# A small load of u moved from the first features' step to the head of the constants (RWKV-6 attention with a hard-swish MLP)

## The chip, the cores and the metric

One core of a Trainium2 chip runs the kernel. The metric is the device time of one execution in microseconds, as the median of several runs. The profile shows one execution; its span is shorter than that execution's time by what lies around it.

## The reference, cut to what matters

Two blocks follow each other. The first is a linear attention with a state that decays: for each batch and head, over 768 steps,

```
cur   = (u * k_t) outer v_t
y_t   = r_t . (state + cur)
state = w_t * state + k_t outer v_t
```

with r, k, v, w of shape (4, 8, 768, 48) and u of shape (8, 48). The part of y that u makes is a number per step and head, the sum over the head's 48 elements of r u k, times v_t. The second block takes y as x of shape (3072, 384): h = x @ w_in, g = h * clip(h + 3, 0, 6) / 6, out = g @ w_out, with w_in of (384, 2048) and w_out of (2048, 384). The weights come as float64.

## The kernel before, in words

**Tiling.** Each sequence is cut into chunks of 128 steps; a chunk i of all 8 heads is one unit of the attention, and there are 24 of them. Every chunk has a chain of steps, each a short function: its features (r, k and w, with 112 partitions of heads' elements) are loaded (feat), two scans on VectorE make the running products of w (back, fore), k and r are scaled by them (K, R), TensorE makes the scores and reads and writes the state (score, read, kv), and ScalarE copies results out of PSUM (kvs, leave). Four chunks make a block of the MLP, whose products (up, down) take most of TensorE's time. The weights are loaded in 16 tiles of 768 KB (fetch, L397), and ScalarE and VectorE turn each from float64 into float32 (low L406, sign L411, shift L417, full L421).

**What u is for.** For the first nine chunks (BY_PE) the diagonal of the scores comes from TensorE: own (L467, VectorE) multiplies r and k into a tile rk, dot (L479, TensorE) multiplies it with u_col, a tile of 112 x 8 numbers that holds u, sum (L485, ScalarE) copies the result to dg, and diag0 and diag1 (L495, ScalarE) put it on the diagonal of A. dot of chunk i is called dot0, dot1 and so on below. rk has one buffer, so the next chunk's own waits for this chunk's dot.

**The order of the work.** It is written out by hand. A planner holds all steps with engine, duration and needs, but their order is a string (ORDER) that gives each step its place, and each engine runs its own in that order. The durations only decide, in a small model inside the plan, how many fillers are put between TensorE's steps of the first 60 us: a filler (spin, L1276) is a product of the identity with itself whose result nobody reads.

TensorE's start reads: 14 fillers (28 matmuls in the profile, which counts two passes for each), dot0, 2 fillers (4), the transposes of K of chunk 0 (turn0, L520), 9 fillers (18), the write of the state (kv0, L620), the scores (L504), dot1, the clearing of y (L674), 7 fillers (14), and the read of chunk 0. turn0 needs a PSUM bank that is free again when sum0 has copied dg; kv0 needs kn of chunk 0 (L528) and its values (v_in).

**Queues.** All loads but one go out from SP: the first weight tile, then w of chunk 0 (260 KB), its r and k (512 KB), the features of chunk 1 (772 KB), the values of chunk 0, the second weight tile, the values of chunk 1, the third weight tile, and the features of chunks 2 and 3. Eight loads at a time can be in flight: each load takes one of eight semaphores in turn, and the ninth waits until the first has landed. The one load that doesn't go out from SP is that of u_col, 112 x 8 floats, 3.5 KB: load_feat(0) issues it on ScalarE's queue (L354), so it stands there behind the table load and the low and sign of the first weight tile.

Of the kernel before, what the change touches and what calls it, by code (L numbers as in the profile page):

```python
# [16 lines left out]
ACT = mybir.ActivationFunctionType  # L17
# [8 lines left out]
BC = 4  # L26
# [220 lines left out]
def fast_path(tc, feat, tok, wflat, ub, ug, moe_w_in, moe_w_out, out, flag, n_chunks):  # L247
# [5 lines left out]
    nc = tc.nc  # L253
# [16 lines left out]
    with ExitStack() as ctx:  # L270
# [17 lines left out]
        plan = Plan()  # L288
# [12 lines left out]
        u_col = const.tile([PR, P, 2], F32, name="u_col")  # L301
# [4 lines left out]

        def constants():

            nc.vector.memset(back, 0.0)
            nc.vector.memset(back[:, :, HL:], 1.0)  # L310
            for b in starts:
                nc.vector.memset(b, 0.0)
            nc.vector.memset(y_ps[:PR, :, P * HL:], 0.0)
            nc.vector.memset(three, 3.0)
            nc.vector.memset(ones, 1.0)
            make_identity(nc, ident)
            nc.gpsimd.tensor_add(eyes, ident[:, :HL], ident[:, HL:])

            mask_f = wk.tile([128, HL], F32, name="clip")
            nc.gpsimd.memset(mask_f, 1.0)  # L320
            for a in range(2):
                nc.gpsimd.affine_select(out=mask_f[a * HL:(a + 1) * HL], in_=mask_f[a * HL:(a + 1) * HL],
                                        compare_op=ALU.is_gt, fill=0.0, base=0, pattern=[[1, HL]], channel_multiplier=-1)
            nc.gpsimd.tensor_copy(out=mask, in_=mask_f)

            for _ in range(4):
                spin()

            new_x(0)
            x3_0 = blocks[0]["x3"]  # L330
            sel = blocks[0]["sel"] = wk.tile([PR, NCC, 128], F32, name="S_", bufs=1)
            nc.gpsimd.memset(x3_0, 0.0)
            nc.gpsimd.memset(sel, 0.0)
            for g in range(2):
                nc.gpsimd.tensor_copy(out=sel[:, :, g * GP + D:g * GP + D + X3],
                                      in_=ident[0:PR, g * GP:g * GP + D].rearrange("q (j r) -> q j r", j=NCC))

        def new_x(bk):

            x = wk.tile([128, NCC + 1, MB], F32, name="xT")  # L340
            blocks[bk].update(xT=x, x3=x[:PR, NCC])
# [7 lines left out]
        def load_feat(i):  # L349
            b = io.tile([feat.shape[1], nf], F32, name="feat_in")  # L350
            a = b[:PR]
            if i == 0:
                nc.sync.dma_start(out=b[:, 2 * n:], in_=feat[chunk_of[i], :, 2 * n:])
                nc.scalar.dma_start(out=u_col, in_=ug)  # L354
            else:
                nc.sync.dma_start(out=b, in_=feat[chunk_of[i]])
            st[i].update(b=b, r=a[:, :n].rearrange("q (x t) -> q x t", t=HL),
                         k=a[:, n:2 * n].rearrange("q (x t) -> q x t", t=HL), w=a[:, 2 * n:])
# [171 lines left out]
        def by_dma(i):  # L530
            return i >= FLIP
# [447 lines left out]
        def do(fn, *args):  # L979
            return lambda: fn(*args)  # L980
# [5 lines left out]
        def when(i):  # L986

            bk, c = divmod(i, BC)
            return BASE[bk] - LAG - (BASE[bk] - BASE[bk - 1]) / BC * (BC - 1 - c) if bk else -99.0
# [8 lines left out]
        def scored(i):  # L998
            return f"score{i}" if i <= BC else f"read{i - 1}"

        def turned_by(i):
            if by_dma(i):
                return f"split{i}"
            return f"turn{i}" if i <= BC + 1 else f"read{i - 2}"
# [4 lines left out]
        def written_by(i):  # L1009
            return f"kv{i}" if i in SOLO else f"read{i - 1}"  # L1010

        for i in range(NT):
            t = when(i)
            k = START[i] if i < len(START) else when(i - 2) - AHEAD
            first, last = is_first(i), is_last(i)
            dve = i < EARLY
            behind = [f"fetch{BEHIND[i]}"] if i < len(BEHIND) and BEHIND[i] >= 0 else []
            plan.add(f"feat{i}", "SP", 0.45 if i else 1.15, do(load_feat, i), behind + [f"feat{i - 1}"] * (i > 0) + ["later"] * (i == 1), k - 20, kb=735 if i else 294,
                     hold=[("feat", [f"K{i}", f"R{i}"] + [f"own{i}"] * (i < BY_PE))])
            plan.add(f"tok{i}", "SP", 0.45, do(load_tok, i), behind + [f"feat{i}"] * (i > 1) + ["later"] * (i < 2), k - 19.9, kb=320,  # L1020
                     hold=[("tok", [read_by(i)])])
# [23 lines left out]
            due = k + 0.7 if i < len(START) else when(i - 1)  # L1045
# [2 lines left out]
                plan.add(f"score{i}", "PE", 0.63, do(score, i), [f"K{i}", f"R{i}"] + [f"score{i - 1}"] * (i > 0), due,  # L1048
                         [("bank", [f"above{i}"])] * 2)
            plan.add(f"above{i}", "DVE", 0.68, do(above, i), [scored(i), f"diag1{i}"], due + 0.5)  # L1050
            if i <= BC + 1:
                plan.add(f"turn{i}", "PE", 0.45, do(turn_k, i), [f"K{i}"] + [f"turn{i - 1}"] * (i > 0), due + 0.01, [("ps", [f"turned{i}"])])
            if by_dma(i):
                plan.add(f"split{i}", "ACT", 0.9, do(split_k, i), [f"K{i}"], due - 6, [("rk", [f"flip{i}"])])
                plan.add(f"flip{i}", "SP", 1.0, do(flip_k, i), [f"split{i}"] + [f"flip{i - 1}"] * by_dma(i - 1), due - 5, [("kvs", [f"turned{i}"])], kb=229)
            plan.add(f"turned{i}", "ACT", 0.8 if by_dma(i) else 0.42, do(turned_k, i), [f"flip{i}" if by_dma(i) else turned_by(i)] + [f"turned{i - 1}"] * (i > 0), due - 2 if i > BC + 1 else due + 0.5,
                     [("kn", [written_by(i)])])
            if i in SOLO:
                plan.add(f"kv{i}", "PE", 0.6, do(write_alone, i), [f"turned{i}", f"tok{i}"], t - 0.2,
# [66 lines left out]
        for f in range(NFC):  # L1126
            for c0, c1 in parts_of[f]:
                m, x = c1 - c0, c0 // BY_SUM
                k = UP[2 * x] + f * UP[2 * x + 1] + (c0 % BY_SUM)
# [35 lines left out]
        for bk in range(NB):  # L1165
            K = BASE[bk]
# [6 lines left out]
            for d in range(2 * (bk > 0)):  # L1173
# [8 lines left out]
                writer, readers, due = {}, {}, {}  # L1182
# [77 lines left out]
        for k, (which, j) in enumerate(vets):  # L1260
            i = 8 + k // 2
# [10 lines left out]
        def spin():  # L1272

            n_ = spins[0] = spins[0] + 1
            at = n_ % 4 * L
            nc.tensor.matmul(still[:, at:at + L], lhsT=ident, rhs=ident, start=n_ == 0, stop=True, skip_group_check=True)  # L1276
# [7 lines left out]
        plan.spin, plan.hint = spin, hint  # L1284
        plan.hint_at = f"down{NB - 1}.1.3.0"
        constants()
        plan.emit()

# [237 lines left out]
def kernel(  # L1526
# [25 lines left out]
    flags = ctx.enter_context(tc.tile_pool(name="flags", bufs=1))  # L1552
    flag = flags.tile([1, 1], I32, name="flag")
    fast_path(tc, feat, tok, wflat, ub, ug, moe_w_in, moe_w_out, out, flag, n_chunks)
    bad = nc.values_load(flag[0:1, 0:1], min_val=0, max_val=128)
    with tc.If(bad > 0, preferred_fallthrough_block=True, label="general"):
# [68 lines left out]
```

## Time and profile before

| | |
|---|---|
| median of 3 runs | 532.97 us (532.53 to 534.28) |
| profiled execution, its own time | 532.08 us |
| its span | 530.3 us |
| TensorE busy | 518.1 us (98%) |
| VectorE busy | 432.5 us (82%) |
| ScalarE busy | 290.4 us (55%) |
| load of u_col: issued, landed after | 5.34 us, 7.05 us |

In the profile PE is TensorE's matmuls, PEld its weight loads, DVE is VectorE, ACT is ScalarE, POOL is GpSimd, SP is SyncE; L12 is line 12 of the kernel before. A timeline row has the start in us, the duration, the engine and line, the operation, the tiles written and read, how many of them, and in brackets the idle time before it with what ended it. The chain of waits is the work that ended last, in order of time: start, duration, what. A DMA row has the issuing queue, how many, the size and the time from issue to landing. Buffer numbers are left out of names: rk of chunk 0 and rk of chunk 1 are both "rk".

### The profile page before, as it was taken

How to read it: one execution, taken by the hardware profiler on the slowest of the kernel's cores; microseconds unless marked ns; L12 is line 12 of the kernel's file. 1: busy time of each engine (PE TensorE's matmuls, PEld its weight loads, DVE VectorE, ACT ScalarE, POOL GpSimd, SP SyncE). 2: the span in 40 equal slices, each digit the busy share in tenths (PEclk: the TensorE clock that was granted, in tenths of full speed). 3: DMA queues.
4: the chain of work that ended last, by engine and by line, in shares of the span. 5: the costliest groups of instructions: out<-in, count | busy, mean ns of one | idle time of the engine just before them, and what ended most of it. 6: DMA issues, size and time to landing. Idle time of an engine off the chain costs nothing.

```text
span 530.3 us, 13609 instructions
## 1 busy us (share of the span) xinstructions
PE 518.1 (98%) x5642; PEld 478.7 (90%) x5642; DVE 432.5 (82%) x762; ACT 290.4 (55%) x680; POOL 86.0 (16%) x79
## 2 busy tenths in 40 slices
PE   4999999999999999999999999999999999999997
PEld 4988889999788999888999988999988999988997
DVE  6699999999799977787996678897789996568951
ACT  2789897445257754587462455665458552334220
POOL 2000000133023043313220503044201300000000
PEclk8899999999999999999999999999999999999999
DMA  8676485035502171454333305433814445453101
GB/s 322 246 297 243 140 284 185 11 90 143 186 2 62 26 199 34 129 183 93 107 99 100 131 20 138 138 100 101 270 33 147 104 151 201 127 197 139 59 11 56
DMA packets 37235, 70.33 MB, mean 133 GB/s; under 512 B 19088, under 2 KB 27184, under 8 KB 37168
## 3 DMA queue, kind: packets, MB, share of 16 engines
q1 hardware_dynamic: 37040, 69.40, 40.7%
q8 instruction: 46, 0.75, 0.6%
q14 instruction: 21, 0.17, 0.1%
q10 hardware_dynamic: 128, 0.00, 0.0%
HBM read 59.69 MB, written 4.72 MB: 121 GB/s over the span
## 4 chain that ended last, share of the span: by engine, by line
PE 88%; DVE 4%; DMA 4%; ACT 2%; SPq 1%; issue 1%; DVEq 0%
PE bank L897 31%; PE bank L840 28%; PE bank L739 7%; PE bankS L897 5%; PE bankS L840 5%; PE y_ps L598 2%; PE bank L504 2%; PE y_ps L607 2%; PE y_ps L620 2%; PE bankS L1276 1%; DMA u_col<-in_ug_dram 1%; DMA feat_in<-in_feat_dram 1%; PE ps L479 1%; DMA bits<-in_moe_w_in_dram 1%; PE ps L520 1%
## 5 line engine op out<-in xcount | busy, mean ns | idle before, releaser
L861 ACT ACTIVATE clip<-g,three 128x512 f32<-128x512 f32 x80 | 56.1, 719 | 49.3 <-DVE g L857 28.2
L857 DVE TENSOR_TENSOR g<-bank,g 128x512 f32<-128x512 f32 x80 | 53.4, 684 | 27.3 <-PE bank L840 23.7
L897 PE MATMUL bank<-w_out,g 128*128 128x192 f32 x384 | 67.4, 327 | 0.0
L897 PEld LDWEIGHTS bank<-w_out,g 128*128 128x128 f32 x384 | 63.3, 190 | 0.5
L865 DVE SCALAR_TENSOR_TENSOR g<-clip,g 128x512 f32<-128x512 f32 x80 | 59.2, 755 | 3.7 <-ACT clip L861 3.7
L495 ACT ACTIVATE A<-eyes,dg 128x64 f32<-128x64 f32 x192 | 49.8, 338 | 0.5 <-DVE dg L487 0.3
L454 POOL TENSOR_TENSOR K<-feat_in,E 112x512 f32<-112x512 f32 x17 | 25.0, 1469 | 151.0 <-DVE E L434 86.9
L855 ACT COPY g<-bank 128x512 f32<-128x512 f32 x50 | 28.8, 585 | 33.5 <-PE bank L840 32.3
L739 PE MATMUL bank<-xT,w_in 128*128 128x256 f32 (+1 forms) x216 | 45.4, 360 | 0.0
L840 PE MATMUL bank<-xT,w_in 128*128 128x256 f32 x160 | 40.2, 379 | 0.3 <-issue 0.3
L739 PEld LDWEIGHTS bank<-xT,w_in 128*128 128x128 f32 x216 | 36.6, 190 | 4.0
L458 POOL TENSOR_TENSOR W<-feat_in,W 112x512 f32<-112x512 f32 x17 | 24.8, 1456 | 94.4 <-DVE W L443 80.8
L706 ACT COPY xT<-y_ps 48x256 f32<-48x256 f32 x88 | 32.2, 366 | 10.4 <-PE y_ps L607 9.5
L915 ACT ACTIVATE o<-bank 128x192 f32<-128x192 f32 x36 | 11.5, 327 | 46.7 <-PE bank L897 46.6
L897 PE MATMUL bankS<-w_out,g 128*128 128x192 f32 x192 | 34.9, 328 | 0.0
L897 PE MATMUL bank<-more,g 128*128 128x192 f32 x192 | 34.3, 329 | 0.0
L840 PEld LDWEIGHTS bank<-xT,w_in 128*128 128x128 f32 x160 | 30.2, 190 | 4.4 <-issue 0.6
L897 PEld LDWEIGHTS bank<-more,g 128*128 128x128 f32 x192 | 31.5, 190 | 0.7
L897 PEld LDWEIGHTS bankS<-w_out,g 128*128 128x128 f32 x192 | 31.6, 190 | 0.2
L470 POOL TENSOR_TENSOR rk<-rk_in 128x384 f32<-128x384 f32 x15 | 17.5, 1164 | 87.2 <-DMA kvs<-rk 39.3
L840 PE MATMUL bank<-xT,bits 128*128 128x256 f32 x120 | 30.7, 380 | 0.0
L443 DVE TENSOR_TENSOR_SCAN W<-feat_in,start 112x520 f32<-112x520 f32 x24 | 30.6, 1273 | 0.0
(306 smaller groups left out, 1128.7 us busy)
## 6 DMA issues: line engine op xcount, KB each, us to landing
feat_in<-in_feat_dram SPq DMA_DIRECT2D x23, 772.5 KB, 5.3
bits<-in_moe_w_in_dram SPq DMA_DIRECT2D x8, 768.0 KB, 6.3
bits<-in_moe_w_out_dram SPq DMA_DIRECT2D x8, 768.0 KB, 5.4
feat_in<-in_moe_w_in_dram SPq DMA_DIRECT2D x8, 768.0 KB, 4.9
feat_in<-in_moe_w_out_dram SPq DMA_DIRECT2D x8, 768.0 KB, 5.3
rk_in<-in_tok_dram SPq DMA_DIRECT2D x15, 384.0 KB, 4.4
v_in<-in_tok_dram SPq DMA_DIRECT2D x24, 192.0 KB, 4.4
feat_in<-in_wflat_dram SPq DMA_DIRECT2D x6, 768.0 KB, 4.7
```

Of the source, the lines that this page charges most:

```text
L443: nc.vector.tensor_tensor_scan(out=W_, data0=d["w"][:, :-1], data1=starts[i % 2].rearrange("q p t -> q (p t)"), initial=0.0, op0=ALU.mult, ...
L454: early(i).tensor_mul(d["K"], d["k"], d["E"][:, :, 1:])
L458: early(i).tensor_mul(d["R"], d["r"], d["R"])
L495: nc.scalar.activation(out=d["A"][:, h, :], in_=eyes, func=ACT.Copy, scale=d["dg"][:, h])
L706: nc.scalar.copy(out=blocks[bk]["xT"][g * GP:g * GP + D, :, at:at + HL], in_=st[i]["y_ps"][a][(g ^ a) * GP:(g ^ a) * GP + D, :, :])
L739: nc.tensor.matmul(h_ps[:, :(c1 - c0) * L], lhsT=w_in[:, f // 2, j, f % 2, :], rhs=b["xT"][:, j, c0 * L:c1 * L], start=(j == 0), stop=(j = ...
L840: nc.tensor.matmul(b["p", d, c][:, z * HB:(z + 1) * HB], lhsT=weight(W_PLACE[r], d)[:, z, :], rhs=x_at(bk, X_PLACE[r]), start=fresh and z ...
L855: nc.scalar.copy(out=out_, in_=src)
L857: nc.vector.tensor_tensor(out=out_, in0=src, in1=out_of(bk, d, other), op=ALU.add if sign > 0 else ALU.subtract)
L861: nc.scalar.activation(out=c, in_=out_of(bk, d, u), func=ACT.Relu, bias=three, scale=twice)
L865: nc.vector.scalar_tensor_tensor(out=g, in0=blocks[bk]["r", d, u], scalar=6.0, in1=g, op0=ALU.min, op1=ALU.mult)
L897: nc.tensor.matmul(b["d", p, to][:, :h], lhsT=a, rhs=w(), start=(f == 0 and k in (1, 5)), stop=(f == HF - 1 and k in (2, 3, 4)), skip_grou ...
```

## The change

The load of u_col becomes the first statement of constants(), which is emitted ahead of all steps, and leaves load_feat. It stays on ScalarE's queue. In the plan the duration of feat0 goes from 1.15 to 0.45, those of split, flip and turned for the later chunks go up a little, and turn is no longer planned for a chunk that is transposed by DMA.

```diff
         def constants():
 
+            nc.scalar.dma_start(out=u_col, in_=ug)
             nc.vector.memset(back, 0.0)
...
             if i == 0:
                 nc.sync.dma_start(out=b[:, 2 * n:], in_=feat[chunk_of[i], :, 2 * n:])
-                nc.scalar.dma_start(out=u_col, in_=ug)
             else:
...
-            plan.add(f"feat{i}", "SP", 0.45 if i else 1.15, do(load_feat, i), behind + [f"feat{i - 1}"] * (i > 0) + ["later"] * (i == 1), k - 20, kb=735 if i else 294,
+            plan.add(f"feat{i}", "SP", 0.45, do(load_feat, i), behind + [f"feat{i - 1}"] * (i > 0) + ["later"] * (i == 1), k - 20, kb=735 if i else 294,
...
-            if i <= BC + 1:
+            if i <= BC + 1 and not by_dma(i):
...
-                plan.add(f"split{i}", "ACT", 0.9, do(split_k, i), [f"K{i}"], due - 6, [("rk", [f"flip{i}"])])
-                plan.add(f"flip{i}", "SP", 1.0, do(flip_k, i), [f"split{i}"] + [f"flip{i - 1}"] * by_dma(i - 1), due - 5, [("kvs", [f"turned{i}"])], kb=229)
+                plan.add(f"split{i}", "ACT", 0.94, do(split_k, i), [f"K{i}"], due - 6, [("rk", [f"flip{i}"])])
+                plan.add(f"flip{i}", "SP", 1.24, do(flip_k, i), [f"split{i}"] + [f"flip{i - 1}"] * by_dma(i - 1), due - 5, [("kvs", [f"turned{i}"])], kb=229)
```

ScalarE's instructions from the start of the program, before and after (the waits name the semaphore of the load that is waited for):

```order
 L1620 UNCONDITIONAL_BRANCH [waits barrier_Pool_Activation_PE_DVE_SP_release]
+L309 DMA u_col<-in_ug_dram 112x8
 L406 ACT_TABLE_LOAD
-L406 ACTIVATE more<-bits 128x768 [waits DMAHW0_49]
-L411 ACTIVATE more<-bits 128x768
-L354 DMA u_col<-in_ug_dram 112x8
+L406 ACTIVATE more<-bits 128x768 [waits DMAHW1_49]
+L411 ACTIVATE more<-bits 128x768
 L461 COPY w_min<-E 112x8 [waits DVE_49]
```

The load moved past the table load and the two conversions of the first weight tile; as it is now the first load of the program, it holds the first semaphore, and the first weight tile the second.

TensorE's instructions around dot0, at the start of the program:

```order
 L1276 MATMUL bankS<-ident 128x128 [waits Pool_49]
 L1276 MATMUL bankS<-ident 128x128 x13
-L479 MATMUL ps<-u_col,rk 64x2 [waits DMAHW4_49,DVE_49]
+L479 MATMUL ps<-u_col,rk 64x2 [waits DMAHW0_49,DVE_49]
 L479 MATMUL ps<-u_col,rk 64x2 x7
 L1276 MATMUL bankS<-ident 128x128 x2
```

Nothing moved here, and the number of fillers is the same all along TensorE's queue; dot0 waits for the same load under another semaphore.

SP's queue from the start of the program, with the chunk's features (feat_in), values (v_in) and weight tiles (bits), after the change:

```order
 L397 DMA bits<-in_moe_w_in_dram 128x768
 L354 DMA feat_in<-in_feat_dram 128x521
 L361 DMA feat_in<-in_feat_dram 128x1024
 L356 DMA feat_in<-in_feat_dram 128x1545
 L368 DMA v_in<-in_tok_dram 128x384
 L397 DMA bits<-in_moe_w_in_dram 128x768
 L368 DMA v_in<-in_tok_dram 128x384
 L397 DMA bits<-in_moe_w_in_dram 128x768 [waits DMAHW0_49]
 L356 DMA feat_in<-in_feat_dram 128x1545 [waits DMAHW1_49]
```

The order of SP's loads and the names in these waits are as before, but the first semaphore is now that of u_col and the second that of the first weight tile, where they were those of the first weight tile and of w of chunk 0.

More of the change, by code (lines that the diff above doesn't have):

```diff
@@ L1050, in fast_path @@
             plan.add(f"above{i}", "DVE", 0.68, do(above, i), [scored(i), f"diag1{i}"], due + 0.5)
-            if i <= BC + 1:
+            if i <= BC + 1 and not by_dma(i):
                 plan.add(f"turn{i}", "PE", 0.45, do(turn_k, i), [f"K{i}"] + [f"turn{i - 1}"] * (i > 0), due + 0.01, [("ps", [f"turned{i}"])])
             if by_dma(i):
-                plan.add(f"split{i}", "ACT", 0.9, do(split_k, i), [f"K{i}"], due - 6, [("rk", [f"flip{i}"])])
-                plan.add(f"flip{i}", "SP", 1.0, do(flip_k, i), [f"split{i}"] + [f"flip{i - 1}"] * by_dma(i - 1), due - 5, [("kvs", [f"turned{i}"])], kb=229)
-            plan.add(f"turned{i}", "ACT", 0.8 if by_dma(i) else 0.42, do(turned_k, i), [f"flip{i}" if by_dma(i) else turned_by(i)] + [f"turned{i - 1}"] * (i > 0), due - 2 if i > BC + 1 else due + 0.5,
+                plan.add(f"split{i}", "ACT", 0.94, do(split_k, i), [f"K{i}"], due - 6, [("rk", [f"flip{i}"])])
+                plan.add(f"flip{i}", "SP", 1.24, do(flip_k, i), [f"split{i}"] + [f"flip{i - 1}"] * by_dma(i - 1), due - 5, [("kvs", [f"turned{i}"])], kb=229)
+            plan.add(f"turned{i}", "ACT", 1.1 if by_dma(i) else 0.42, do(turned_k, i), [f"flip{i}" if by_dma(i) else turned_by(i)] + [f"turned{i - 1}"] * (i > 0), due - 2 if i > BC + 1 else due + 0.5,
                      [("kn", [written_by(i)])])
```

## The prediction

> **What bounds the kernel now.** I read the page's busy shares first, then the chain of waits from the start to 24 us, then the timelines of DVE and ACT over the same stretch, the granted clock by stretches, and last the landing times of single loads. The page's first part says that TensorE is the engine that counts:
>
> ```profile
> PE 518.1 (98%) x5642; PEld 478.7 (90%) x5642; DVE 432.5 (82%) x762; ACT 290.4 (55%) x680; POOL 86.0 (16%) x79
> ```
>
> PE is busy for 518.1 of 530.3 us, so only some 12 us of the span have no matmul in them. The chain of waits (start us, duration us, what) shows that one load of 3.5 KB stands in the largest hole:
>
> ```profile
> 5.34 7.05 DMA u_col<-in_ug_dram
> 12.40 0.14 issue
> 12.53 1.02 PE ps L479 x16
> 13.56 1.16 PE bankS L1276 x4
> 14.71 0.75 PE ps L520 x4
> 15.46 2.72 PE bankS L1276 x18
> 18.18 0.51 PE y_ps L620 x32
> ...
> 19.16 0.56 PE ps L479 x16
> ...
> 20.79 1.56 PE bankS L1276 x14
> ...
> 23.69 0.55 PE ps L520 x4
> ...
> 34.70 0.57 PE y_ps L620 x31
> ```
>
> The load of u is issued at 5.34, lands 7.05 us later, and 0.14 us after that the first products with it (dot0, L479) run. PE's own row of dot0 in the timeline gives the hole (the bracket is the idle time before it):
>
> ```profile
> 12.53 1.02 PE L479 MATMUL ps<-u_col,rk 112*64 112x2 f32 x16 [5.28 <-DMA u_col<-in_ug_dram]
> ```
>
> So PE stands from 7.25 to 12.53. Two more things are in these rows. The same 16 matmuls of L479 take 1.02 us at 12.53 and 0.56 at 19.16; four transposes of L520 take 0.75 at 14.71 and 0.55 at 23.69; 14 fillers of L1276 take 1.56 at 20.79 (0.111 each), while 18 took 2.72 before. The granted clock by stretches says why (stretch, length, busy times, PEclk, DMA share, GB/s):
>
> ```profile
> 7.30:9.90 2.60, 0.00 (x0) 0.00 (x0) 2.29 (x5) 0.23 (x2) 0.00 (x0) 1.00 0.97 371
> 10.00:12.40 2.40, 0.00 (x0) 0.00 (x0) 1.75 (x3) 0.00 (x0) 0.00 (x0) 0.50 1.01 404
> 12.50:16.70 4.20, 4.17 (x31) 4.18 (x32) 2.05 (x3) 2.60 (x10) 0.00 (x0) 0.50 1.00 416
> 17.00:24.00 7.00, 6.91 (x161) 6.26 (x160) 4.74 (x10) 4.50 (x13) 0.00 (x0) 1.00 0.34 132
> ```
>
> The clock fell to 0.50 in the hole and stayed there to about 16.7. The hole costs its own length and then a stretch at half clock.
>
> **The change part by part.**
>
> *The load goes to the head of ACT's queue.* Before, it stood behind the first two conversions, the first of which waits for its weight tile to 5.33 (ACT's rows below). Now ACT issues it first, at about 0.8, where its first instruction is now. What dot0 needs besides u is rk of chunk 0 from DVE:
>
> ```profile
> 7.86 0.69 DVE L467 TENSOR_TENSOR rk<-feat_in 112x512 f32<-112x512 f32 x1 [0.28 <-DMA feat_in<-in_feat_dram]
> ...
> 11.07 0.68 DVE L458 TENSOR_TENSOR W<-feat_in,W 112x512 f32<-112x512 f32 x1
> 13.59 0.69 DVE L467 TENSOR_TENSOR rk<-feat_in 112x512 f32<-112x512 f32 x1 [1.84 <-PE ps L479]
> ...
> 19.26 0.36 DVE L550 TENSOR_TENSOR S<-kvs,w_min 112x192 f32<-112x192 f32 x1 [3.58 <-ACT kvs L631]
> ```
>
> rk is ready at 8.55. Even if u took the same 7.05 us from its new issue it would land at 7.9, so its landing time need not be known: dot0 starts when rk is there, at 8.55 + 0.14 = 8.69. Gain so far 12.53 - 8.69 = 3.84 us.
>
> *The clock.* The hole shrinks from 5.28 to 8.69 - 7.25 = 1.44 us. I take it that the clock stays at full. Then from dot0 to the first write into the state (kv0, L620) PE needs 0.56 + 4 x 0.111 + 0.55 + 18 x 0.111 = 3.56 us, where it took 1.02 + 1.16 + 0.75 + 2.72 = 5.65. Gain 2.09, together 5.93: kv0 at 12.25 in place of 18.18. The trace has no hole of 1.4 us at this place, so the bounds of this term are 0 and 2.09; I take 2.09, since the clock was still at 1.00 to 9.9, 2.6 us into the long hole. The Trainium skill (TensorE: Matmul & The Clock Gate, section HAM oscillation) has the rule that gaps above about 3.4 us make the array fall back to half rate; by that rule a hole of 5.28 falls back, as the trace shows, and one of 1.44 does not, and the sum would be the same 5.93. The same page (Part 1) says that the window is free-running and shifts from run to run; by that some runs would keep only part of the 2.09, which no run here shows yet.
>
> *What is late next, on ACT.* Between dot0 and kv0 ACT must copy dg, build the diagonal and copy kn:
>
> ```profile
> 0.80 1.28 ACT L406 ACT_TABLE_LOAD   x1 [0.80 <-PEq L1611]
> 5.33 1.08 ACT L406 ACTIVATE more<-bits 128x768 uint16<-128x768 uint32 x1 [3.25 <-DMA bits<-in_moe_w_in_dram]
> ...
> 13.59 0.17 ACT L485 COPY dg<-ps 128x8 f32<-128x8 f32 x1 [6.02 <-PE ps L479]
> 13.86 2.02 ACT L495 ACTIVATE A<-eyes,dg 128x64 f32<-128x64 f32 x8
> 15.78 0.51 ACT L528 COPY kn<-ps 128x448 f32<-128x448 f32 x1
> 18.75 0.48 ACT L631 COPY kvs<-y_ps 112x384 f32<-112x384 f32 x1 [2.46 <-PE y_ps L620]
> 19.13 1.08 ACT L406 ACTIVATE more<-bits 128x768 uint16<-128x768 uint32 x1
> ```
>
> dg starts 0.04 after dot0's end (12.53 + 1.02), so at 9.29, and kn ends 15.78 + 0.51 - 13.59 = 2.70 later, at 11.99: 0.26 before PE asks. ACT is then free for kvs, which follows PE and ends at 19.23 - 5.93 = 13.30. The table load now stands behind the issue of u; an issue takes 0.47 in SP's row below, so it ends near 2.6 instead of 2.1. The first conversion waits for its tile to 5.33, so this edit costs nothing; its cover is 2.7 us.
>
> *On DVE.* The scaled r (L458) is ready at 11.75 and doesn't move. rk of chunk 1 no longer waits 1.84 for dot0's bank and starts at 11.75, if its features are there. That load, issued between 2.1 and 2.5, took 7.5 us:
>
> ```profile
> feat_in<-in_feat_dram SPq DMA_DIRECT2D x1, 772.5 KB, 7.5
> ```
>
> It lands by 10.0, so rk is ready at 12.44, before dot1 at 19.16 - 5.93 = 13.23. The scan and reciprocal of chunk 1 follow it; DVE was done with them at 19.26 - 3.58 = 15.68, now 1.84 earlier, at 13.84, which is after kvs: the state's first step (L550) starts at 13.84, 5.4 us earlier, not 5.9. PE reads that state behind its 14 fillers, at 22.35 before and 16.4 now, so the 0.5 us are hidden.
>
> *Loads that keep their time.* The first burst of loads is bound by bandwidth (404 and 416 GB/s above) and lands when it did. The tightest is the second weight tile, for the conversion at 19.13, now due at 13.20:
>
> ```profile
> 3.36 0.47 SPq L397 DMA_DIRECT2D bits<-in_moe_w_in_dram  x1
> ```
>
> ```profile
> bits<-in_moe_w_in_dram SPq DMA_DIRECT2D x1, 768.0 KB, 9.7
> ```
>
> 3.36 + 9.7 = 13.06: just in time.
>
> Later loads are issued when a buffer comes free, so they move with the engines. The one without slack is the values of chunk 2, issued between 28.5 and 28.8, which land some 0.1 before PE starts with them (34.70, in the chain above):
>
> ```profile
> v_in<-in_tok_dram SPq DMA_DIRECT2D x1, 192.0 KB, 6.0
> ```
>
> *SP's queue.* Its order is the same, but its eighth load waits for a semaphore that u now holds, and its ninth for that of the first weight tile: both go out a little earlier. They stand behind six loads of the same queue that are in flight until 13, so they land as before: nothing. The changed durations in the plan's table change no instruction's place and no number of fillers: nothing.
>
> **The sum.** 3.84 + 2.09 = 5.93 us. From kv0 on every engine is in the same relation as before, and PE has no waits of size until the end, so I carry it to the end whole. The profiled execution took 532.08 (span 530.3, and 1.8 around it), which makes 526.2; the median of the runs is 0.9 above it, so from 532.97 it makes 527.0.
>
> **The rivals.**
> *The clock falls anyway* (0.12). The stretch around the hole is too idle and PE runs the next one at half rate. Against: the hole is a quarter of the old. For: the shares at which the clock turns aren't in this trace. Then only the waiting goes: 532.97 - 3.84 = 529.1.
> *The loads set the pace* (0.09). The fifth weight tile is now asked for while the first burst still runs (DMA share 1.00 to 16.7), and pushes the values of chunk 2 back by one tile, 786 KB at 416 GB/s = 1.9 us. For: that load has no slack. Against: DMA share is 0.34 between 17 and 24. Gain 4.0, 529.0.
> *Nothing is left* (0.04). The same load keeps its old landing time of 34.6 whatever is issued when, and PE waits there for all that it won: 533.0. Against: its issue is chained to ACT's conversions, which move.
> *Slower* (0.03). The table load, now behind the DMA, is held up by the burst of loads. If it ended at T, two conversions of 1.08, the copy of dg (0.2), the transposes (0.75) and 18 fillers at half clock (2.72) would follow, and kv0 would be at T + 5.8: from T = 12.4 on that is later than 18.18. The longest landing in the burst, of a load issued between 5.9 and 6.2, is this one:
>
> ```profile
> feat_in<-in_feat_dram SPq DMA_DIRECT2D x1, 772.5 KB, 11.3
> ```
>
> With it T = 1.2 + 11.3 + 1.3 = 13.8, kv0 at 19.6, 1.4 slower and 534.4; held up somewhat longer, it passes the bound. Against: the table load took 1.28 before, beside SP's first issue.
>
> **How the numbers follow.** The forecast has 0.72, 527.0. A measurement of this kernel can tell about 0.3%, 1.6 us, from no change. The first two rivals are faster by more than that too: faster 0.72 + 0.12 + 0.09 = 0.93, same 0.04, slower 0.03. The range goes from 525.8 (the profiled execution's 526.2, less 0.4 for sums of rounded rows) to 529.8 (the first two rivals, and 0.7 for a clock that returns later still).
>
> **What would show it.** Right: u issued before 1.3 us; PE's idle time before dot0 near 1.4 and ended by DVE's rk, not by a DMA; the clock at 1.00 between 8.7 and 17; 16 matmuls of L479 in about 0.56 at 8.7; kv0 near 12.3; L620 of chunk 2 near 28.8. Wrong: u landing after 8.6; a clock of 0.50 after 8.7 (first rival); idle time before L620 of chunk 2, ended by the values' load (second and third); a table load that ends after 5.3 (slower).

## The result, and the profile after

The changed kernel takes 529.69 us (median of nine runs, 527.37 to 531.58); the kernel before took 533.46 beside it (nine runs, 532.53 to 534.60). The ratio is 0.9924, 95% interval 0.9904 to 0.9944: faster by 3.8 us, where 5.9 were forecast. The profiled execution took 528.87 with a span of 527.1, 3.2 less than that of before.

The busy shares hardly differ from those of before, as a change of 4 us in 530 must look there; the start is where to look. Timelines of ACT and DVE of the kernel after (start, duration, engine and line, tiles), and the row of its load of u:

```profile
0.81 0.42 ACTq L309 DMA_DIRECT2D u_col<-in_ug_dram  x1
1.25 1.28 ACT L406 ACT_TABLE_LOAD   x1 [1.25 <-PEq L1611]
...
11.20 0.51 ACT L528 COPY kn<-ps 128x448 f32<-128x448 f32 x1
...
12.96 1.07 ACT L406 ACTIVATE more<-bits 128x768 uint16<-128x768 uint32 x1
```

```profile
7.61 0.67 DVE L467 TENSOR_TENSOR rk<-feat_in 112x512 f32<-112x512 f32 x1
...
11.40 0.69 DVE L467 TENSOR_TENSOR rk<-feat_in 112x512 f32<-112x512 f32 x1
...
13.39 0.31 DVE L550 TENSOR_TENSOR S<-kvs,w_min 112x192 f32<-112x192 f32 x1
```

```profile
u_col<-in_ug_dram ACTq DMA_DIRECT2D x1, 3.5 KB, 4.7
```

u lands at 0.81 + 4.7 = 5.5, before rk is there. PE's timeline of the kernel after, first around dot0 and kv0, then around the write of chunk 2 (kv2, the second L620):

```profile
8.33 0.63 PE L479 MATMUL ps<-u_col,rk 112*64 112x2 f32 x16 [0.93 <-DVE rk L467]
8.89 0.71 PE L1276 MATMUL bankS<-ident 128*128 128x128 f32 x4
...
9.83 2.19 PE L1276 MATMUL bankS<-ident 128*128 128x128 f32 x18
11.95 0.57 PE L620 MATMUL y_ps<-v_in,kn 64*48 64x48 f32 x32
...
27.03 1.45 PE L682 MATMUL bank<-xT,S__117 112*128 112x64 f32 x12
29.52 0.57 PE L620 MATMUL y_ps<-v_in,kn 64*48 64x48 f32 x32 [1.03 <-ACT xT L689]
...
30.59 1.51 PE L1276 MATMUL bankS<-ident 128*128 128x128 f32 x6
31.89 2.59 PE L739 MATMUL bank<-xT,w_in 128*128 128x256 f32 x6
```

kv0 starts at 11.95, 6.2 us earlier. But 17 us on there is a hole of 1.03 that before did not have, and behind it the same 6 matmuls of L739 that need 1.46 us elsewhere (a row of a later run, below) take 2.59. The granted clock by stretches of the kernel after (stretch, length, busy times, clock, DMA share, GB/s) says why:

```profile
6.90:10.20 3.30, 2.37 (x33) 2.16 (x32) 3.27 (x6) 1.89 (x7) 0.00 (x0) 1.00 1.02 408
...
17.00:24.00 7.00, 7.00 (x151) 6.64 (x148) 6.58 (x12) 5.94 (x14) 0.00 (x0) 1.00 0.81 305
...
27.40:30.70 3.30, 2.27 (x59) 2.09 (x59) 3.27 (x8) 3.25 (x10) 0.00 (x0) 1.00 0.99 393
30.80:34.10 3.30, 3.30 (x12) 2.78 (x11) 1.11 (x2) 0.64 (x4) 0.00 (x0) 0.50 0.99 403
34.30:40.00 5.70, 5.70 (x61) 4.92 (x60) 5.14 (x11) 5.48 (x13) 0.00 (x0) 1.00 0.34 117
```

The clock held in the smaller hole ahead of dot0 and fell at 30.8 instead, for one stretch. The DMA share between 17 and 24 is 0.81, where it was 0.34 before: the next weight tile is asked for at 16.91 instead of 22.84, while the first burst still runs (its last load lands at 21.15). The rows of the two loads that SP issues at 22.1 and 22.6, of u once more as a broadcast over partitions (u_bc, used from chunk 9 on) and of chunk 2's values:

```profile
u_bc<-in_ub_dram SPq DMA_DIRECT2D x1, 192.0 KB, 6.7
v_in<-in_tok_dram SPq DMA_DIRECT2D x1, 192.0 KB, 6.8
```

The values are issued at 22.60, 6.0 us earlier than before, and take 6.8 us where they took 6.0, so they land at 29.4, 0.14 before kv2. Over their flight the DMA share is 0.90, where it was 0.82 (a stretch of after, then one of before):

```profile
22.60:29.40 6.80, 5.79 (x84) 5.04 (x83) 6.77 (x13) 6.57 (x20) 0.00 (x0) 1.00 0.90 306
28.60:34.60 6.00, 5.86 (x84) 5.11 (x84) 5.97 (x11) 5.89 (x18) 0.00 (x0) 1.00 0.82 294
```

Pairing the matmuls of the two traces one by one, fillers left out, gives how far PE is ahead of the kernel before along the program:

| at (us, before) | ahead by (us) | what happened since the row above |
|---|---|---|
| 12.53, dot0 | 4.20 | the wait for u is gone |
| 18.11, kv0 | 6.16 | full clock from dot0 to kv0 |
| 34.70, kv2 | 5.18 | hole ahead of kv2 |
| 37.62, L739 | 3.59 | half clock behind it |
| 64.71 | 3.84 | steps of about 0.2 and less |
| 135.51, L840 | 2.99 | one new wait, below |
| 526.63, last | 3.21 | |

The wait at 135.51 is in PE's row of the kernel after, and the kernel before has none there:

```profile
132.52 1.10 PE L840 MATMUL bank<-xT,bits 128*128 128x256 f32 x4 [0.84 <-DMA xT<-xT]
```

### The profile page after: what moved, and what is told of

It reads as the page before. It is cut to its first block, busy times and chain, and to the rows that moved or that the text cites. A ratio compares the mean times of both kernels' runs of the same rounds, so it can differ in the third digit from the quotient of the medians.

```text
span 527.1 us, 13608 instructions
## 1 busy us (share of the span) xinstructions
PE 517.7 (98%) x5642; PEld 477.7 (91%) x5642; DVE 431.6 (82%) x762; ACT 290.1 (55%) x680; POOL 86.7 (16%) x79
## 4 chain that ended last, share of the span: by engine, by line
PE 86%; DVE 6%; DMA 3%; SPq 2%; ACT 1%; issue 1%; DVEq 0%
PE bank L897 29%; PE bank L840 28%; PE bank L739 8%; PE bankS L897 5%; PE bankS L840 5%; PE y_ps L598 2%; PE bank L504 2%; PE y_ps L607 2%; PE y_ps L620 2%; DMA feat_in<-in_feat_dram 1%; PE bankS L1276 1%; PE ps L479 1%; DMA bits<-in_moe_w_in_dram 1%; SPq L713 1%; DVE E L434 1%
## 5 line engine op out<-in xcount | busy, mean ns | idle before, releaser
L739 PE MATMUL bank<-xT,w_in 128*128 128x256 f32 (+1 forms) x216 | 46.7, 366 | 0.0
L739 PEld LDWEIGHTS bank<-xT,w_in 128*128 128x128 f32 x216 | 37.4, 194 | 4.5 <-issue 0.3
L840 PE MATMUL bank<-xT,w_in 128*128 128x256 f32 x160 | 40.1, 379 | 0.0
L840 PEld LDWEIGHTS bank<-xT,w_in 128*128 128x128 f32 x160 | 30.2, 190 | 3.8
L434 DVE TENSOR_TENSOR_SCAN E<-feat_in,back 112x520 f32<-112x520 f32 x24 | 29.9, 1245 | 2.8 <-DMA feat_in<-in_feat_dram 2.8
L840 PE MATMUL bank<-xT,bits 128*128 128x256 f32 x120 | 30.7, 380 | 0.8 <-DMA xT<-xT 0.8
```

The lines of the kernel that those rows point to most:

```text
L434: nc.vector.tensor_tensor_scan(out=E_[:, ::-1], data0=d["w"][:, :0:-1], data1=back.rearrange("q p t -> q (p t)")[:, ::-1], initial=0.0, op ...
L739: nc.tensor.matmul(h_ps[:, :(c1 - c0) * L], lhsT=w_in[:, f // 2, j, f % 2, :], rhs=b["xT"][:, j, c0 * L:c1 * L], start=(j == 0), stop=(j = ...
L840: nc.tensor.matmul(b["p", d, c][:, z * HB:(z + 1) * HB], lhsT=weight(W_PLACE[r], d)[:, z, :], rhs=x_at(bk, X_PLACE[r]), start=fresh and z ...
```

## The experiments

All of them use two edits. One moves a step in the planner's order to stand right behind another; it goes ahead of the line that sorts the steps by rank. The other puts extra fillers ahead of a step of TensorE. "tok2" is the load of chunk 2's values, "fetch3" that of weight tile 3, the sixth to go out, "u" the load of u_bc. In the changed kernel SP's order is fetch3, the values of chunk 3, u_bc, tok2, the features of chunk 4.

```diff
+        place = {n: k for k, n in enumerate(steps)}
+        for n, behind in {'tok2': 'fetch3'}.items():
+            rank[place[n]] = rank[place[behind]] + 0.5
...
+            for _ in range({'dot0': 6}.get(n, 0)):
+                self.spin()
```

Theory A: the forecast gain is won up to kv0, and what is lost again is the late load of chunk 2's values with the clock's fall behind it. Against it stands the first rival of the prediction: the clock falls in what is left of the hole ahead of dot0. The letters B and C in the expectations stand for other rivals, which each expectation names itself. Lines move by a few in these kernels; L479 is L482 in the first and so on.

**1. The changed kernel with the values first.**

```diff
+        for n, behind in {'tok2': 'fetch3'}.items():
```

> The changed kernel, with the load of chunk 2's values put ahead of chunk 3's and of u_bc on SP's queue. Theory A (what the change wins up to kv0, 6.2 us, is lost again where PE waits for chunk 2's values: 1.0 us of waiting and 1.5 us of half clock behind it): the values land near 26, PE doesn't wait at 28.5, kv2 starts near 28.5, the clock stays at 1.00 to 34, the span is some 2.5 us below the changed kernel's 527.1, so near 524.6, and the median some 6 us below the kernel before. Rival B (the loads as a whole set the pace, and the wait only goes to the next load): PE or VectorE waits as long for the next load, the features of chunk 4, and the time is that of the changed kernel within 0.5 us.

Measured: 529.14 (526.23 to 531.43, six runs; before 533.49), ratio 0.9916 (0.9882 to 0.9949). In its profile the values are no longer waited for (L623 starts at 31.91, straight behind L685), but the clock fell ahead of dot0, where the kernel is the same as the changed one. A row of PE's timeline and two stretches of the clock:

```profile
8.78 0.87 PE L482 MATMUL ps<-u_col,rk 112*64 112x2 f32 x16 [1.98 <-DVE rk L470]
```

```profile
5.60:9.00 3.40, 1.42 (x19) 1.23 (x17) 2.84 (x5) 2.09 (x3) 0.00 (x0) 1.00 1.02 415
9.00:12.40 3.40, 3.40 (x28) 3.38 (x26) 3.40 (x5) 2.60 (x10) 0.00 (x0) 0.50 1.04 413
```

The runs fall apart into 526.2 to 527.9 and 530.3 to 531.4, so the time alone decides nothing, and the 6 us below the kernel before that A expected of the median came out as 4.4. The run does show that the fall ahead of dot0 happens in some runs.

**2. The kernel before with the values first.** The same move, against the kernel before.

```diff
+        for n, behind in {'tok2': 'fetch3'}.items():
```

> The kernel before, with the same two loads exchanged. Theory A (this load was just in time before, and became late only by the change): no change, within 0.3 us. Rival (it was a bound before as well, only hidden in the rows): faster by 1 us or more.

Measured: 533.35 (532.11 to 535.96, twelve runs), ratio 1.0015 (0.9997 to 1.0033). PE's timeline of this run around kv2:

```profile
33.61 1.45 PE L685 MATMUL bank<-xT,S__116 112*128 112x64 f32 x12
34.99 0.57 PE L623 MATMUL y_ps<-v_in,kn 64*48 64x48 f32 x32
```

No change, as A has it: in the kernel before the load had just enough time, so there an earlier one is worth nothing.

**3. The kernel before with 20 more fillers ahead of dot0** (against the kernel before). u is as late as ever, but PE is kept busy while it waits. This takes the clock's term alone.

```diff
+            for _ in range({'dot0': 20}.get(n, 0)):
+                self.spin()
```

> The kernel before, with 20 more fillers (40 matmuls, 4.5 us at full clock) ahead of dot0, so that PE works through most of the wait for u, which stays. Theory A (the forecast's two terms are apart: 3.84 us of waiting and 2.09 us of half clock): dot0 stays at 12.5, the clock stays at 1.00, the way from dot0 to kv0 falls from 5.6 to 3.6, kv0 is near 16.1, and the time falls by 2 us. Rival (the clock returns so soon, or what is behind has so much slack, that it costs nothing by itself): no change.

Measured: 529.29 (528.78 to 530.68, six runs; before 533.49), ratio 0.9934 (0.9912 to 0.9955). PE's timeline of this run:

```profile
11.85 0.63 PE L481 MATMUL ps<-u_col,rk 112*64 112x2 f32 x16 [1.07 <-DMA u_col<-in_ug_dram]
...
15.46 0.57 PE L622 MATMUL y_ps<-v_in,kn 64*48 64x48 f32 x32
```

The clock never fell. From dot0 to kv0 it is 3.61 us, which is the 3.56 that the prediction summed up, against 5.6 before. The gain of 4.2 is more than the 2.1 of that term: u landed 0.7 earlier in this run, and the prediction read the term from one execution, of 532.08 and with a mean granted clock of 0.994, while the runs of before beside this experiment have a median of 533.49 and mean clocks of 0.989 to 0.994: some of them lost more. With fillers alone, and u as late as ever, the kernel before is as fast as the changed one, within the noise.

**4. The changed kernel with six fillers ahead of kv2.** The load stays late; the hole is filled.

```diff
+            for _ in range({'kv2': 6}.get(n, 0)):
+                self.spin()
```

> The changed kernel, with 6 more fillers (1.3 us at full clock) ahead of kv2, where PE waited 1.0 us for the values of chunk 2. Theory A (1.5 of the lost 2.5 us are the clock that falls behind that wait): the wait stays inside the fillers, kv2 starts near 29.6, the clock stays at 1.00, and the span is some 1.3 us below 527.1. Rival C (the fall of the clock at 30.8 has another cause, such as the small matmuls there, or comes by chance from run to run): the clock falls all the same and the time is the same or up to 0.3 us longer.

Measured: 527.88 (526.01 to 528.85, six runs; before 533.49), ratio 0.9897 (0.9871 to 0.9922). In the profile kv2 starts at 30.19, 0.67 later than in the changed kernel, and the six matmuls of L741 behind it (L739 there) take 1.46:

```profile
30.19 0.57 PE L622 MATMUL y_ps<-v_in,kn 64*48 64x48 f32 x32
...
32.34 1.46 PE L741 MATMUL bank<-xT,w_in 128*128 128x256 f32 x6
```

So the half clock comes from the hole: with the hole filled it is gone, although kv2 starts later, and PE ends 4.9 us ahead of the kernel before in place of 3.2. In the changed kernel it costs more (1.6) than the wait itself (1.0).

**5. The changed kernel with six fillers ahead of dot0.** This guards the first hole only.

```diff
+            for _ in range({'dot0': 6}.get(n, 0)):
+                self.spin()
```

> The changed kernel, with 6 more fillers ahead of dot0, in the hole of 0.9 to 2 us that is left there. Theory A (which of its runs are slow is decided by whether the clock falls in that hole, as in the profile with chunk 2's values first, where it fell at 9.0, or behind the wait for those values): the clock never falls before dot0, kv0 is near 12 to 12.5, the slow runs above 530.5 go, and the median is 1 us or more below the changed kernel's, some 4.5 to 5 us below the kernel before. Rival (the spread of the changed kernel is that of its loads): the same median and the same spread of 4 us.

Measured: 527.82 (526.62 to 530.63, seven runs; before 533.16), ratio 0.9907 (0.9875 to 0.9939). The profiled execution took 530.37. Its chain of waits around kv2, and its clock by stretches:

```profile
23.66 7.22 DMA v_in<-in_tok_dram
30.88 0.14 issue
31.01 0.89 PE y_ps L622 x32
...
34.43 2.56 PE bank L741 x6
```

```profile
27.60:30.90 3.30, 2.04 (x19) 1.90 (x18) 3.27 (x7) 3.24 (x9) 0.00 (x0) 1.00 0.96 341
31.00:37.80 6.80, 6.79 (x92) 5.68 (x92) 2.77 (x6) 2.49 (x8) 0.00 (x0) 0.50 0.89 357
```

With the first hole filled, the second loss is there alone and larger: the load took 7.22, the chain names it, and the clock fell behind it for two stretches. This is A's loss without a fall ahead of dot0. The runs above 530.5 were expected to go; one of 530.63 stayed.

**6. Fillers at both places.**

```diff
+            for _ in range({'dot0': 6, 'kv2': 6}.get(n, 0)):
+                self.spin()
```

> The changed kernel with 6 more fillers ahead of dot0 and 6 ahead of kv2. Theory A: both places are covered, the clock stays at 1.00 from its first rise to the end, the median is some 6 us below the kernel before and no run is above 529. Rival (loads alone): as with the fillers ahead of kv2 alone, 5.6 us below, with the same spread.

Measured: 527.19 (525.59 to 528.45, six runs; before 533.16), ratio 0.9891 (0.9862 to 0.9921). Five of six runs kept the clock. In the profiled one it fell at 32.6 all the same, behind a hole of 1.36 in the middle of dot3 for which the profile shows no releaser:

```profile
32.27 0.40 PE L481 MATMUL ps<-u_col,rk 112*64 112x2 f32 x7 [1.36 <-issue]
```

**7. The changed kernel once more**, beside the kernels of 5, 6 and 8, to see whether the loss at kv2 repeats.

> The changed kernel once more, for a second profile of it. Theory A: the small hole ahead of dot0 is ended by rk and lasts 0.9 to 2.2 us, and the clock either falls at its end or doesn't, depending on where the 3.4 us stretches by which it is set happen to lie; where it falls, kv0 is near 14 to 15.5 and the time above 530; where it doesn't, kv0 is near 12. PE waits for chunk 2's values if kv0 is near 12. Rival: kv0 near 12 and the clock at 1.00 up to 30 in every run.

Measured: 528.35 (one run). Chain of waits of that run:

```profile
29.83 0.57 PE y_ps L620 x31
...
32.70 2.04 PE bank L739 x6
```

The values were issued at 23.21 and landed at 29.69, kv2 came 0.14 later, and the clock was at 0.50 from 30.66 to 34.07. It repeats.

**8 and 9. Both causes taken away, twice:** the values first, u_bc later, and six fillers ahead of dot0.

```diff
+        for n, behind in {'tok2': 'fetch3', 'u': 'fetch9'}.items():
+            rank[place[n]] = rank[place[behind]] + 0.5
...
+            for _ in range({'dot0': 6}.get(n, 0)):
+                self.spin()
```

> The changed kernel with 6 more fillers ahead of dot0, chunk 2's values ahead of chunk 3's, and u_bc (needed from chunk 9 on) loaded some 25 us later, so that there is nothing to wait for at kv2 and no filler is spent there. Theory A: PE doesn't wait at kv2, which starts near 28.6; the median is some 6.5 us below the kernel before, 0.5 us better than with fillers at both places. Rival B (the loads as a whole set the pace): the wait moves to the features of chunk 4 or to the weight tiles behind them, and the median stays 4.5 to 5 us below the kernel before.

> The version with chunk 2's values earlier, u's broadcast load later and six fillers ahead of dot0, once more, beside the same version without the fillers on the same chip. If the fillers keep the clock from falling in the hole ahead of dot0: most runs at a mean granted clock of 0.999 or more, median 526 to 527. If they do nothing: the same spread as the version without them, 526 to 530, median near 528.

Measured: 526.60 (525.48 to 527.24, six runs; before 533.16), ratio 0.9881 (0.9853 to 0.9909); and again 526.62 (526.12 to 527.10, five runs; before 533.16), ratio 0.9886 (0.9864 to 0.9907). PE's timeline of the second of them:

```profile
3.73 4.88 PE L1281 MATMUL bankS<-ident 128*128 128x128 f32 x30
8.53 0.63 PE L484 MATMUL ps<-u_col,rk 112*64 112x2 f32 x16
...
29.31 0.57 PE L625 MATMUL y_ps<-v_in,kn 64*48 64x48 f32 x32
...
31.25 1.46 PE L744 MATMUL bank<-xT,w_in 128*128 128x256 f32 x6
```

No hole ahead of dot0, none ahead of kv2 (the values landed at 27.4), and the clock stayed at 1.00. So the wait didn't move on to another load, as rival B had it. In the two profiles PE ends 5.3 and 5.7 us ahead of the kernel before. This version has the lowest median of all, and its eleven runs lie within 1.8 us, where nine of the changed kernel spread over 4.2.

**10 and 11. The order of the loads without the fillers, twice.**

```diff
+        for n, behind in {'tok2': 'fetch3', 'u': 'fetch9'}.items():
+            rank[place[n]] = rank[place[behind]] + 0.5
```

> The changed kernel with chunk 2's values issued right behind chunk 3's weight tile and the broadcast load of u put back behind the tenth weight tile; no extra spins anywhere. Theory A (the late values and the clock's fall behind them are what was lost again; extra spins ahead of the first features' matmul only guard against a fall of the clock there): the values land near 27, TensorE does not wait for them, median 526.3 to 527.6, single runs 2 to 4 us longer. Theory B (the spins are what made the version with both edits fast, the order of the loads is worth nothing): 529 to 530, as the changed kernel itself.

> The version with chunk 2's values earlier and u's broadcast load later, no fillers. If the hole ahead of dot0 is what makes it vary: runs in two groups, near 526.4 at a mean granted clock of 0.999 or more and 528.5 to 530 at 0.997 or less, with several in each. If the fillers in the other version do nothing, the two kernels have the same two groups in the same shares.

Measured: 528.82 (526.35 to 530.11, six runs; before 533.21), ratio 0.9907 (0.9879 to 0.9936); and 528.39 (527.00 to 531.58, eight runs; before 533.16), ratio 0.9912 (0.9877 to 0.9946). The median that I expected of A for the first, 526.3 to 527.6, was missed, and so was that of the rival there, 529 to 530. What A called "single runs" is more than half of them. The two profiles show why. First the run of 526.54, PE's timeline, a row of ACT's, and the clock by stretches:

```profile
8.38 0.63 PE L482 MATMUL ps<-u_col,rk 112*64 112x2 f32 x16 [2.07 <-DVE rk L470]
...
28.54 0.57 PE L623 MATMUL y_ps<-v_in,kn 64*48 64x48 f32 x32
```

```profile
28.87 0.64 ACT L692 COPY xT<-bank 64x192 f32<-64x192 f32 x2
```

```profile
4.60:7.90 3.30, 1.72 (x15) 1.52 (x14) 2.14 (x4) 2.06 (x3) 0.00 (x0) 1.00 1.04 422
8.00:11.30 3.30, 2.92 (x37) 2.90 (x38) 3.30 (x5) 2.14 (x10) 0.00 (x0) 1.00 1.02 402
```

Then the run of 530.24 of the same kernel, the same views:

```profile
8.61 1.02 PE L482 MATMUL ps<-u_col,rk 112*64 112x2 f32 x16 [1.99 <-DVE rk L470]
...
11.32 4.07 PE L1279 MATMUL bankS<-ident 128*128 128x128 f32 x18
15.32 0.62 PE L623 MATMUL y_ps<-v_in,kn 64*48 64x48 f32 x32
```

```profile
5.30:8.60 3.30, 1.32 (x12) 1.13 (x11) 2.61 (x5) 2.08 (x3) 0.00 (x0) 1.00 1.02 420
8.70:12.00 3.30, 3.30 (x28) 3.29 (x29) 3.30 (x5) 2.23 (x10) 0.00 (x0) 0.50 1.05 416
```

The same kernel and the same hole, 2.07 and 1.99 us. In one run it was divided over two stretches of the clock and cost nothing; in the other it lay in one stretch, with PE busy for 1.32 of 3.30, and the next two were at half. In the first run PE is 6.1 us ahead of the kernel before at kv0 and still 5.7 at the last matmul: there the gain is carried to the end. The first run also settles a name in the profile: kv2 starts at 28.54, ahead of the two copies of L692 (L689 in the changed kernel) at 28.87, so the "ACT xT L689" that the changed kernel's row names is not what kv2 waits for. It happened to end when the values landed.

**The runs by granted clock.** Every run has a mean granted clock. A stretch of 3.4 us at half takes 1.7 us of 527 off it, that is 0.003, so 0.999 and above is a run without such a stretch and 0.997 one with one:

| kernel | runs at 0.999 or more: number, median us | runs at 0.997 or less: number, median us |
|---|---|---|
| before, beside the experiments | 0 | 53, 533.2 to 533.5 in the four sets of runs |
| before, fillers ahead of dot0 (3) | 6, 529.3 | 0 |
| the changed kernel (with 7) | 0 | 10, 529.3 |
| values first (1) | 3, 527.2 | 3, 530.4 |
| values first, u_bc later (10, 11) | 5, 527.0 | 9, 529.5 |
| fillers ahead of dot0 (5) | 4, 526.8 | 3, 530.4 |
| fillers ahead of kv2 (4) | 5, 527.4 | 1, 528.4 |
| fillers at both (6) | 5, 526.7 | 1, 528.5 |
| values first, u_bc later, fillers ahead of dot0 (8, 9) | 11, 526.6 | 0 |

Whichever edit is made to the changed kernel, its runs without a fall have medians of 526.6 to 527.4, and those with at least one 1 to 4 us more. The changed kernel as it is never ran without one.

## Why the prediction was right and where it was wrong

**The start came out step by step.** u issued at 0.81 (said: before 1.3); dot0 at 8.33 (8.69), its hole 0.93 (1.44) and ended by rk, which came 0.3 earlier than before; the clock at 1.00 to 17; kv0 at 11.95 (12.25). The term of the wait was 4.20 (3.84) and that of the clock 1.96 (2.09), together 6.16 (5.93). On ACT kn ended at 11.71 (11.99) and did not hold kv0; on DVE rk of chunk 1 came at 11.40 (11.75), and the state's first step at 13.39 (13.84). The table load ended at 2.53 (2.6), so the rival that ends slower has no ground. The second weight tile, issued at 3.53, landed at 11.9, 1.1 before its conversion at 12.96; "just in time" was too careful.

**The step that failed** is in the sum: "From kv0 on every engine is in the same relation as before, and PE has no waits of size until the end, so I carry it to the end whole." The engines were; the loads were not. The prediction had named the values of chunk 2 as the load without slack and held that loads issued when a buffer comes free move with the engines. The issue did move, by 6.0 us. The landing moved by 5.2, because the load took 0.8 longer, with a DMA share of 0.90 over its flight in place of 0.82. That is the outcome that the second rival named, at half of its size, 1.0 us in place of 1.9. Its mechanism isn't shown: the fifth weight tile, which was to push the values back, landed at 23.04, 0.4 after they were issued. What the prediction held against that rival, a DMA share of 0.34 between 17 and 24, was read at times that the change itself moves. By itself the wait cost 1.0 us.

**What made it dear is the first rival at another place.** The clock fell "anyway", but not in the hole ahead of dot0 that the prediction weighed: in the profiled run it fell 22 us later, behind the hole that the late load made, and took 1.6 us. The prediction priced the two rivals apart and at one place each; the run had both, the one setting off the other. Experiments 4, 5 and 8 show that pair: fill the second hole and the fall behind it is gone, fill only the first and the second loss stays, take both away and the whole forecast gain is there (6.5 us in the medians, 0.6 more than forecast).

**The number** held in part by luck. The measured 529.69 is 2.7 above the forecast of 527.0 and 0.1 inside the range, whose upper end was set for either rival alone and 0.7 more. What happened is the two together, and single runs went up to 531.58.

**The first rival itself has its share too.** In one profile each of experiments 1 and 11, whose program is the changed kernel's up to dot0 and beyond, the clock fell ahead of dot0 for two stretches; in the four other profiles with that program (the changed kernel, 4, 7 and 10) it held. The chance of 0.12 for it looks too low, for a reason that the trace of before could not show: its one phase of the clock's stretches. The prediction's own argument, that the clock was still at 1.00 2.6 us into the long hole, tells only that the stretch in which that hole began lasted to 9.97. The Trainium skill (TensorE: Matmul & The Clock Gate, section HAM oscillation) has the rule that only gaps above about 3.4 us lead to half rate. The prediction leaned on it beside its own reading, and these runs disagree, since the clock fell behind holes of 1.99 and 1.03 us. What the same page of the Trainium skill says in Part 1, a window of 3.4 us that runs freely and lies differently in each run, the traces bear out: the first rise came anywhere from 4.29 to 7.09 in thirteen profiles.

**What stays open.** Where the clock fell in the runs that were only timed isn't known; their mean clock tells only that it did. Why the load of chunk 2's values took longer isn't settled either: in the five profiles with the changed kernel's order of loads (after, 4, 5, 6 and 7) it took 5.9 to 7.2 us. The 0.84 us that PE waits at 132.52 of the changed kernel's profile, by its row for a DMA of xT, has no cause shown; the runs of 526.54 and of experiment 7 don't have it.

## What to carry to other kernels

A gain at the start is carried to the end only if the loads behind it have slack: list the loads that land just in time, and ask of each whether the DMA engines are free at the earlier time, not only whether its issue moves. A short new wait can cost more through the clock than by its length, so price the two together, and keep TensorE busy with a few fillers wherever a wait of 1 us or more is left, above all where the matmuls around it are small. A kernel whose runs spread over 4 us where its neighbour's spread over 2 is telling of such a lottery; the mean granted clock of each run sorts them.

## What the runs showed of the hardware

The clock is granted in stretches of 3.41 us: the fall of the changed kernel lasts from 30.77 to 34.18, and falls of two stretches 6.82 or 6.83. Their phase differs from run to run. How long PE is busy in a stretch doesn't decide by itself what follows. Ahead of dot0, 1.32 and 1.42 of about 3.3 us were followed by half clock, 1.67 and 1.72 were not (experiments 11, 1, 2 and 10). But behind 2.27 of 3.30 ahead of kv2 it fell, and in experiment 7 behind 2.35.

What decides in these traces is how much of TensorE's array the matmuls use. PE's rows tell it: 64*48 64x48 of kv2 is a matmul on 64 rows and 48 columns of the array, through which 48 columns stream. Let each matmul count 128 x 128 parts as one, times its streamed columns: a filler counts 128, a matmul of kv2 9, one of dot0 0.9. Summed over the stretches of all thirteen traces, from the first rise of the clock on, the 15 at full clock that half clock followed have 0 to 1473, and the 1953 that full clock followed have 1603 or more. At half clock, the five that half clock followed have up to 1486, the eight that full clock followed 1687 or more. A stretch of fillers alone has some 3900, an estimate from 0.111 us for each. The stretch with the hole ahead of kv2 has 878 in the changed kernel, since the matmuls behind that hole are small; the one with the hole ahead of dot0 has 1796. This border was found in the traces afterwards, and no run was made to test it.

A load of 3.5 KB issued at the head of the program, on a queue of its own and at the same moment as the first weight tile, took 4.7 us to land, hardly less than the 768 KB tile's 4.8. Behind the queued burst it had taken 7.05, and 6.4 and 6.5 in experiments 3 and 2.
